# W_down weight sums: one pair of F tiles per gate/up pair, GpSimd's part tied to product ends, a new ring order

## The chip, the cores and the metric

The kernel runs on one core of a Trainium2 chip. The metric is the device time of one execution in microseconds (us), the median of several runs; lower is better. A ratio in this text is the mean time of one kernel's fast runs over that of the other kernel's fast runs of the same rounds, so it isn't quite the ratio of the medians that stand beside it. An interval is a 95% interval of such a ratio.

Short names: PE is TensorE (its matmuls), PEld its weight loads, DVE is VectorE, ACT is ScalarE, POOL is GpSimd, SP is the sequencer that issues nearly all DMAs, in program order.

## The reference, cut to what matters

The model is a linear-attention block and then a gated MLP, both with a layernorm in front. Only the MLP matters here (S = 2048 tokens, D = 1024, F = 3584, bf16):

```python
gate = x @ W_gate                  # D x F
up   = x @ W_up                    # D x F
h    = relu(gate) * up
out  = residual + h @ W_down       # F x D
```

The kernel does it in two passes of 1024 tokens. A pass has a gate/up stage, in 14 *pairs* of F tiles, and a *down* stage. Both use a fast matrix product of seven block products (P1 to P7, in the order P1, P5, P6, P2, P7, P3, P4) instead of eight; parts of the down stage use it at two levels. Fewer matmuls are paid for with sums of weight blocks. Those of W_down are made once, in pass 0, beside the gate/up matmuls, written to scratch in HBM and read back by both down stages.

## The kernel before: the parts that matter

For each pair `q` a raw 512 KB block of W_down is loaded into one of two buffers (`wraw`). VectorE makes four sums of it (`wd_sums`), then, for every two pairs, four second-level sums (`wl_sums`, two halves); GpSimd makes four more straight from the raw blocks (`raw`). All three are stored.

```python
def wd_sums(q):                       # VectorE, 4 subtractions from wraw into wsum, then a store (t_scr)
    ...
def wl_sums(m):
    def half(i): ...                  # VectorE, 2 + 2 subtractions from wsum; then a store (l_scr)
    def addw(j, x, y):                # GpSimd
        PL.add("pool", lambda e: e.tensor_tensor(..., op=ALU.subtract), reads=x[1] + y[1], ...)
    def raw():
        addw(0, ...); addw(2, ...); addw(1, ...); addw(3, ...)
        dma(..., "st_wm_%d" % m)      # the store (l_scr)
```

A pair calls lists of such functions at fixed places of its seven products: `mid[0]` before P2, `mid[2]` inside P2, `mid[3]` before P3, `mid[1]` before P4. Late layernorm tiles of the next pass also run here, in pairs 3 to 10.

```python
wt_at = {q: [q] for q in range(NPAIR - 1)}
wt_at[NPAIR - 2].append(NPAIR - 1)          # pair 12 makes the sums of pairs 12 and 13
...
for x in wt_at.get(q, []):
    mid[1 if q == 0 else 0].append(lambda x=x: wd_sums(x))
    if x % 2 == 1:
        w0_, w1_, wr_ = wl_sums(x // 2)
        mid[1].append(w0_); wl_q.append(w1_); mid[0].append(wr_)
        # then the raw loads of the next two pairs, also in mid[0]
if q not in wt_at:                           # pair 13: no sums, all seven ring loads
    mid[0] += wl_q + [load_wd_next] * NWS
```

The down stage reads its weights through a *ring* of seven slots. A load may start when its slot is free; from then on each finished product starts the load seven places ahead. Slots 0 to 3 lie over `wraw` and `wsum`, so they are free when the last sums are done. Slot 4 lies over GpSimd's sums, slots 5 and 6 over the late layernorm tiles, which are done two pairs before the end. At the end of every pair SP also issues two gate/up loads of 512 KB each.

Of the kernel before, what the change touches and what calls it, by code (L numbers as in the profile page):

```python
# [132 lines left out]
def bass_sequential_preLN__linear_attn_block__glu_gated_reglu__prompt_kernel(  # L133
# [72 lines left out]
    with es:  # L206
# [143 lines left out]
        def bank(b, w=512):  # L350
            return ps[:, b, 0:w]
# [100 lines left out]
        def flat(x):  # L452
            return [b for row in x for b in (flat(row) if isinstance(row, list) else [row])]
# [20 lines left out]
            b_.over = B_wo  # L474
        for b_ in B_wd[0:NWS - 3]:
            b_.over = B_wraw + flat(B_wsum)
        for b_ in flat(B_lsw):
            b_.over = flat(B_xnT) + flat(B_pqT)
        B_wd[NWS - 3].over = flat(B_lsw)
# [60 lines left out]
        def dma(slot, dst_ap, src_ap, name, reads=(), writes=(), eng="sp"):  # L540
            return PL.add(eng, lambda e: e.dma_start(dst_ap, src_ap), reads=reads, writes=writes, slot=slot,  # L541
                          name=name)
# [52 lines left out]
        for src in WSRC:  # L595
            if src[0] == "l":
                WLIST += [("l", src[1]) + x for x in LSRC]
            else:
                WLIST += [src + c for c in WCH]

        X_AT = [(NPAIR - 3) * 2 + i for i in range(NWX)]
        RING = [list(range(NWS))]
        RING.append([(len(WLIST) + i) % NWS for i in range(NWS)] +
                    [NWS + (NPAIR * 2 + x) % NWG for x in X_AT])

        def wd_slot(L):
# [57 lines left out]
        def wl_sums(m):  # L664
            z = m % 2
            no = len(L2O)
            oa = slice(L2O[0], L2O[-1] + 1)

            def wq_(k, h):
                return wsum[:, (2 * m + k) % NWR, oa, h * HNW:(h + 1) * HNW], \  # L670
                    [B_wsum[(2 * m + k) % NWR][o] for o in L2O]

            def t(j):
                return lsum[:, z, :, j, :], [B_lsum[z][j]]

            def add(j, x, y):
                PL.add("dve", lambda e: e.tensor_tensor(out=lsum[:, z, :, j, :], in0=x[0], in1=y[0],
                                                        op=ALU.subtract),
                       reads=x[1] + y[1], writes=[B_lsum[z][j]], name="WL%d_%d" % (j, m))

            def half(i):
                if i == 0:
                    add(0, wq_(0, 1), wq_(0, 0))
                    add(2, wq_(1, 1), wq_(0, 1))
                else:
                    add(1, wq_(1, 1), t(0))
                    add(3, wq_(1, 0), t(1))
                    dma(sl_ls[z], l_v[:, 0:no, :, m, :], lsum[:, z], "st_wl_%d" % m, reads=B_lsum[z],
                        writes=[B_lscr[m]])
            def wr(k, h):  # L690
                return wraw[:, (2 * m + k) % NWR, 1, NW + h * HNW:NW + (h + 1) * HNW], [B_wraw[(2 * m + k) % NWR]]

            def addw(j, x, y):
                PL.add("pool", lambda e: e.tensor_tensor(out=lsw[:, z, j, :], in0=x[0], in1=y[0], op=ALU.subtract),
                       reads=x[1] + y[1], writes=[B_lsw[z][j]], name="WM%d_%d" % (j, m))

            def raw():
                def t_(j):
                    return lsw[:, z, j, :], [B_lsw[z][j]]
                addw(0, wr(0, 1), wr(0, 0))  # L700
                addw(2, wr(1, 1), wr(0, 1))
                addw(1, wr(1, 1), t_(0))
                addw(3, wr(1, 0), t_(1))
                dma(sl_lw[z], l_v[:, no, :, m, :], lsw[:, z], "st_wm_%d" % m, reads=B_lsw[z], writes=[B_wscr[m]])
            return [lambda: half(0), lambda: half(1), raw]

        def mm(out_ap, lhsT, rhs, start, stop, reads, bbuf, name, skip=False):
# [600 lines left out]
        def strassen_pair(ps_, q, fill, mid):  # L1308
# [16 lines left out]
            def s_blk(i):  # L1325
                return (lambda kk: Ssum[:, i, kk, :]), [B_S[i]]

            def w_blk(w, k, h):
                return (lambda kk: wring[:, iw[w], k * KH + kk, h * P:(h + 1) * P]), [B_w[iw[w]]]

            def t_blk(w, j):
                return (lambda kk: Tring[:, kt[w], j, kk, :]), [B_T[kt[w]][j]]

            def prod(w, b, st_, mov, start, name):
                (sf, sr), (mf, mr) = st_, mov
                for kk in range(KH):
                    mm(bank(b), sf(kk), mf(kk), start and kk == 0, kk == KH - 1, sr + mr, B_bank[b],
                       "%s%s_%d_%d" % (name, "gu"[w], ps_, q), skip=True)

            def add_s5(dst, src, bsrc, w, bdst, name):  # L1340
                PL.add("dve", lambda e: e.tensor_tensor(out=dst, in0=src, in1=ftmp[:, w, :], op=ALU.add),  # L1341
                       reads=[bsrc, B_s5[w]], writes=[bdst], name=name)
# [29 lines left out]
            fillin(1)  # L1372
            for w in range(2):
                prod(w, BB[w], t_blk(w, 2), s_blk(2), False, "P7")
                add_s5(c22[:, w, :], bank(BB[w]), B_bank[BB[w]], w, B_c22[w], "c22")
            relu(c22[:, 0, :], c22[:, 0, :], [], B_c22[0], "rl22")
            for f_ in mid[3]:
                f_()
            for w in range(2):
                prod(w, BC_[w], w_blk(w, 1, 1), s_blk(3), False, "P3")  # L1380
                add_s5(c12[:, w, :], bank(BC_[w]), B_bank[BC_[w]], w, B_c12[w], "c12")
                if w == 0:
                    mul(hh[:, f2, SBW:2 * SBW], c22[:, 0, :], c22[:, 1, :], B_c22, B_hh[f2][1], "hh22")
# [25 lines left out]
        def down_pass(ps_, fill):  # L1409
# [253 lines left out]
            def at(pi, ci, *fs):  # L1663
                post.setdefault((pi, ci), []).extend(fs)
# [26 lines left out]
            for i, f_ in enumerate(sg4 + sg3):  # L1691
                at(4, i // 2, f_)
            order = (2, 3, 0, 1)
            at(5, 0, *[lambda j=j: add_h(V_, B_V, 1, 0, j) for j in order], *[lambda j=j: p_22(j) for j in range(STB)],
               lambda: e_u5(0), lambda: e_u5(1))
            at(5, 1, lambda: e_u5(2), lambda: e_u5(3))
            at(5, 4, st_flush)
            for f_, places in fill:
                at(*places, f_)
# [194 lines left out]
        wl_q = []  # L1894
        ln_q = []
        LQ = 3
        wt_at = {q: [q] for q in range(NPAIR - 1)}
        wt_at[NPAIR - 2].append(NPAIR - 1)

        for p_ in range(NPASS):  # L1900
            fill = []
            for q in range(NPAIR):
                if q + 1 < NPAIR:
                    fill = fill + t_sums((p_ * NPAIR + q + 1) * 2)
                if q > 0:
                    hh_sums(q - 1)
                mid = [[], [], [], []]
                if p_ == 0:
                    mid[2] += ln_q
                    ln_q.clear()  # L1910
                    if q == LQ - 1:
                        mid[2] += [lambda: late_load(0), lambda: late_load(1)]
                    if LQ <= q < LQ + TPP:
                        m_, sq_, n_ = late_steps(q - LQ)
                        mid[2].append(m_)
                        mid[3].append(sq_)
                        ln_q.append(n_)
                    for x in wt_at.get(q, []):
                        mid[0] += wl_q
                        wl_q.clear()  # L1920
                        mid[1 if q == 0 else 0].append(lambda x=x: wd_sums(x))
                        if x % 2 == 1:
                            w0_, w1_, wr_ = wl_sums(x // 2)
                            mid[1].append(w0_)
                            wl_q.append(w1_)
                            mid[0].append(wr_)
                            for z in (x + 1, x + 2):
                                if z < NPAIR:
                                    mid[0].append(lambda z=z: load_wraw(z))
                    if q not in wt_at:  # L1930
                        mid[0] += wl_q + [load_wd_next] * NWS
                        wl_q.clear()
                strassen_pair(p_, q, fill, mid)
                if p_ == 1 and q >= NPAIR - 3:
                    load_wd_next()
                    load_wd_next()
            assert not fill
            hh_sums(NPAIR - 1)
            late = []
            if p_ + 1 < NPASS:  # L1940
                slots_ = [(0, 1), (0, 3), (2, 0), (2, 1), (2, 2), (2, 3), (4, 1), (4, 2)]
                late = [(lambda t=t: late_t(t), slots_[t]) for t in range(TPP)]

                def nxt_t():
                    claim(flat(B_T[0:2]), B_sgo)
                    claim(flat(B_T[2:4]), B_sgo + B_dsum)

                def nxt_s():
                    claim(B_S, [B_D2])
                ss = s_sums()  # L1950
                ts = t_sums((p_ + 1) * NPAIR * 2)
                late += [(nxt_t, (3, 1))] + [(ts[i], (3, 2 + i)) for i in range(4)]
                late += [(nxt_s, (4, 4))] + [(ss[i], (6, (0, 0, 1, 2)[i])) for i in range(4)]
            down_pass(p_, late)
# [53 lines left out]
```

## Time and profile before

| | before |
|---|---|
| median (first 3 runs) | 736.23 us (735.11 to 737.95) |
| span of the profiled run | 734.9 us |
| PE busy | 98% |
| a gate/up pair with no wait | 12.08 us for 56 matmuls of 512 columns |
| pairs of pass 0 that cost more | 12.23, 12.53 and 13.18 us |
| down stage of pass 0 (from the last pair's P4) | 82.53 us |

The page of before, parts 1 (busy time, share of the span, instructions) and 4 (the chain that ended last, share by engine), one line of each:

```profile
PE 720.8 (98%) x4253; PEld 363.2 (49%) x4311; DVE 561.6 (76%) x976; ACT 352.0 (48%) x614; POOL 103.7 (14%) x169
...
PE 82%; DVE 9%; DMA 3%; issue 2%; ACT 2%; SPq 1%; POOL 1%; POOLq 0%; DVEq 0%; ACTq 0%
```

TensorE sets the pace. What a change of the sums can reach is the time in which PE waits. Before, the view of waits for PE from 225 us to the end (who waited for whom: us in total, times, longest) has three lines:

```profile
PE ps L710 <- DVE RE L1341: 1.6, 2, 1.1
PE ps L710 <- DVE RAB L1423: 1.0, 1, 1.0
PE ps L710 <- DMA RW<-in_B_W_down_dram: 0.4, 1, 0.4
```

The first is at 266 and 388 us in the gate/up stage; the other two come near 470 us, at the end of the down stage. Three us in all. The cause of the longest stall in the gate/up stage is seen in the timeline of before (start, duration, engine, line, operation, tile out <- in, forms, count; in brackets the idle time in front of it and what ended it):

```profile
377.88 0.84 POOL L694 TENSOR_TENSOR RAB<-RW 128x256 f16<-128x256 bf16 x1 [10.43 <-DMA RW<-in_B_W_down_dram]
...
380.60 1.15 DVE L1289 TENSOR_TENSOR RO<-RWG 128x1024 f16<-128x1024 bf16 x1
...
383.21 3.01 DVE L655 TENSOR_TENSOR RW<-RW 128x512 f16<-128x512 bf16 x8
...
388.30 1.67 PE L710 MATMUL ps<-RH,RO 128*128 128x512 bf16 x7 [1.14 <-DVE RE L1341]
```

Eight first-level sums in a row (L655) took VectorE 3.01 us, where a pair with four takes 1.55 us when nothing slows them. A T sum (L1289) took 1.15 us beside GpSimd; undisturbed it takes 0.68 us. PE then waits 1.14 us for VectorE's addition from PSUM.

### The profile page before, as it was taken

The page shows a single profiled execution, that of the slowest core. Times are in us where ns is not written, and L with a number is a line of the kernel's source. Part 1 is how long each engine was busy: PE and PEld are TensorE (multiplying, and loading weights), DVE is VectorE, ACT ScalarE, POOL GpSimd, SP SyncE. Part 2 cuts the span into 40 slices and gives each one's busy share as a digit, 9 for nine tenths or more (in the row PEclk, how much of TensorE's full clock was granted, in tenths as well). Part 3 has the DMA queues.
Part 4 walks back from the last instruction along what each step waited for, and adds up shares of the span by engine and source line. Part 5 has one row for each costly group of instructions (what it writes and reads, how often), then busy time and mean ns, then how long its engine had stood idle before and what let it go on. Part 6 is the DMA issues. An engine that isn't in the chain of part 4 may idle for free.

```text
span 734.9 us, 11505 instructions
## 1 busy us (share of the span) xinstructions
PE 720.8 (98%) x4253; PEld 363.2 (49%) x4311; DVE 561.6 (76%) x976; ACT 352.0 (48%) x614; POOL 103.7 (14%) x169
## 2 busy tenths in 40 slices
PE   8999999999999999999999999999999999999998
PEld 3444444344444444444444666754444444447766
DVE  7878877898775999898997769865757575667594
ACT  4877666764832456777754100135454544521000
POOL 1311100000450112132320003400000000000052
PEclk9999999999999999999999999999999999999999
DMA  9644154024999889888969999982323242327892
GB/s 313 202 91 83 29 142 157 3 30 75 214 228 260 234 258 272 241 243 256 300 198 305 318 247 336 311 263 79 101 71 109 63 116 58 100 92 245 246 314 87
DMA packets 191880, 133.93 MB, mean 182 GB/s; under 512 B 51664, under 2 KB 173776, under 8 KB 191824
## 3 DMA queue, kind: packets, MB, share of 16 engines
q1 hardware_dynamic: 191152, 132.54, 63.6%
q8 instruction: 34, 0.56, 0.3%
q10 hardware_dynamic: 672, 0.66, 0.3%
q14 instruction: 22, 0.18, 0.1%
HBM read 96.47 MB, written 25.17 MB: 166 GB/s over the span
## 4 chain that ended last, share of the span: by engine, by line
PE 82%; DVE 9%; DMA 3%; issue 2%; ACT 2%; SPq 1%; POOL 1%; POOLq 0%; DVEq 0%; ACTq 0%
PE ps L710 82%; DMA RW<-in_B_W_down_dram 1%; DVE RAB L796 1%; DVE RE L1171 1%; ACT RX L789 1%; DMA RX<-h_scr 1%; DVE st L724 1%; DMA RAB<-RXH 1%; DVE RX L793 1%; SPq L541 1%; DVE RX L1012 1%; DVE RO L1289 1%; POOL rstd L734 0%; DVE RW L906 0%; ACT ps L715 0%
## 5 line engine op out<-in xcount | busy, mean ns | idle before, releaser
L715 ACT ACTIVATE ps<-ps 128x512 f32<-128x512 f32 x172 | 100.1, 582 | 213.5 <-PE ps L710 162.0
L710 PE MATMUL ps<-RC,RO 128*128 128x512 f16 x672 | 154.3, 379 | 0.0
L710 PE MATMUL ps<-RH,RWG 128*128 128x512 bf16 x447 | 105.6, 379 | 0.1
L710 PEld LDWEIGHTS ps<-RC,RO 128*128 128x128 f16 x672 | 65.7, 98 | 79.5 <-ACT ps L715 0.5
L1345 DVE TENSOR_TENSOR RAB<-ps,RAB 128x512 bf16<-128x512 f32 x56 | 38.6, 689 | 71.9 <-PE ps L710 71.9
L710 PE MATMUL ps<-RC,RWG 128*128 128x512 f16 x320 | 76.8, 379 | 0.3 <-ACT ps L715 0.3
L1341 DVE TENSOR_TENSOR RE<-ps,RE 128x512 bf16<-128x512 f32 x112 | 74.2, 684 | 1.6 <-PE ps L710 0.7
L710 PEld LDWEIGHTS ps<-RH,RWG 128*128 128x128 bf16 x448 | 43.9, 98 | 52.6
L710 PE MATMUL ps<-RW,RAB 128*128 128x256 f16 (+3 forms) x412 | 66.8, 318 | 1.5 <-DVE RAB L1423 1.0
L1423 POOL TENSOR_TENSOR RE<-RE,RX 128x512 f32<-128x512 f32 x16 | 23.1, 1473 | 307.5 <-DMA RX<-h_scr 307.5
L715 ACT ACTIVATE RE<-RE 128x512 bf16<-128x512 bf16 x56 | 35.1, 627 | 65.0 <-DVE RE L1341 64.4
L710 PE MATMUL ps<-RH,RO 128*128 128x512 bf16 (+1 forms) x228 | 55.3, 379 | 3.0 <-DVE RE L1341 1.6
L710 PE MATMUL ps<-RW,RE 128*128 128x512 bf16 x243 | 56.6, 380 | 1.5 <-DVE RXH L1195 0.7
L710 PE MATMUL ps<-RAB 128*128 128x512 bf16 (+2 forms) x268 | 57.6, 351 | 0.4
L715 ACT ACTIVATE RE<-ps 128x512 f32<-128x512 f32 x64 | 37.6, 597 | 35.4 <-PE ps L710 35.0
L710 PEld LDWEIGHTS ps<-RW,RAB 128*128 128x128 bf16 (+1 forms) x414 | 40.4, 98 | 25.8 <-DVE RAB L1423 1.3
L710 PEld LDWEIGHTS ps<-RC,RWG 128*128 128x128 bf16 (+1 forms) x320 | 30.0, 98 | 40.2 <-ACT ps L715 6.2
L1289 DVE TENSOR_TENSOR RO<-RWG 128x1024 f16<-128x1024 bf16 x54 | 39.7, 736 | 4.7 <-DMA RWG<-in_B_W_up_dram 4.7
L1423 DVE TENSOR_TENSOR RE<-ps,RE 128x512 f32<-128x512 f32 x40 | 27.0, 687 | 18.9 <-PE ps L710 15.6
L715 ACT ACTIVATE RAB<-ps 128x512 bf16<-128x512 f32 x56 | 33.4, 596 | 14.7 <-PE ps L710 13.6
L710 PEld LDWEIGHTS ps<-RH,RO 128*128 128x128 f16 (+1 forms) x256 | 24.2, 98 | 31.8 <-DVE RE L1341 2.2
L710 PEld LDWEIGHTS ps<-RAB 128*128 128x128 bf16 (+1 forms) x274 | 26.3, 98 | 25.2 <-ACT RAB L856 1.1
(138 smaller groups left out, 994.0 us busy)
## 6 DMA issues: line engine op xcount, KB each, us to landing
RWG<-in_B_W_gate_dram SPq DMA_DIRECT2D x28, 512.0 KB, 5.0
RWG<-in_B_W_up_dram SPq DMA_DIRECT2D x28, 512.0 KB, 5.9
RW<-in_B_W_down_dram SPq DMA_DIRECT2D x14, 512.0 KB, 6.1
t_scr<-RW SPq DMA_DIRECT2D x14, 512.0 KB, 3.5
RE<-in_A_x_dram SPq DMA_DIRECT2D x23, 256.0 KB, 3.5
RW<-l_scr SPq DMA_DIRECT2D x13, 448.0 KB, 6.3
l_scr<-RX SPq DMA_DIRECT2D x7, 768.0 KB, 4.4
RW<-in_B_W_down_dram SPq DMA_DIRECT2D x12, 384.0 KB, 5.0
```

The costliest lines, as they stand in the source:

```text
L541: return PL.add(eng, lambda e: e.dma_start(dst_ap, src_ap), reads=reads, writes=writes, slot=slot, name=name)
L710: lambda e: e.matmul(out_ap, lhsT, rhs, start=start, stop=stop, skip_group_check=skip),
L715: PL.add("act", lambda e: e.activation(out=dst, in_=src, func=func), reads=reads, writes=writes, name=name)
L724: PL.add("dve", lambda e: e.bn_stats(out=st6[:, k, c * 6:(c + 1) * 6], in_=src_full[:, c * BCH:(c + 1) * BCH]), reads=[src_chunk_bufs[c]], ...
L789: PL.add("act", lambda e: e.activation(out=Et[:, k, :], in_=src, func=ACTF.Exp), reads=[src_buf], writes=[B_E[k]], name=name + "_exp")
L793: PL.add("dve", lambda e: e.tensor_scalar(out=Et[:, k, :], in0=Et[:, k, :], scalar1=1.0, scalar2=1e-6, op0=ALU.min, op1=ALU.add), reads=[] ...
L796: PL.add("dve", lambda e: e.scalar_tensor_tensor(out=dst_ap, in0=src, scalar=C1, in1=Et[:, k, :], op0=ALU.add, op1=ALU.max), reads=[src_bu ...
L1012: PL.add("dve", lambda e: e.tensor_tensor(out=s_, in0=p_, in1=s_, op=ALU.add), reads=[pb], writes=[sb_], name=name + "_add")
L1289: PL.add(eng, lambda e: e.tensor_tensor(out=tb(j, u), in0=f0(u), in1=f1(u), op=ALU.subtract), reads=[B_w[i + x] for x in r] + ([B_T[k + x] ...
L1341: PL.add("dve", lambda e: e.tensor_tensor(out=dst, in0=src, in1=ftmp[:, w, :], op=ALU.add), reads=[bsrc, B_s5[w]], writes=[bdst], name=name)
L1345: PL.add("dve", lambda e: e.tensor_tensor(out=dst, in0=a_, in1=b_, op=ALU.mult), reads=reads, writes=[wr], name=name)
L1423: PL.add(eng, lambda e: e.tensor_tensor(out=dst, in0=in0, in1=in1, op=op), reads=reads, writes=writes, name=name)
```

## The change

The intent: spread the sums evenly (pair 13 makes its own), keep GpSimd out of VectorE's way by letting each of its four subtractions start only at the end of a P7 or P3 product, when VectorE adds from PSUM, and make up for the later sums by filling the ring in the order in which slots come free (5, 6, 0, 1, 2, 3, 4). Four U5 additions of the down stage also move ahead of a wait. The core of the diff:

```diff
+        for b_ in B_wd[0:2]: b_.over = list(B_wraw)      # ring slots 0 and 1 wait for wraw alone
...
-        RING = [list(range(NWS))]
+        RING = [[NWS - 2, NWS - 1] + list(range(NWS - 2))]
...
             def addw(j, x, y):
                 PL.add("pool", ...,
-                       reads=x[1] + y[1], ...)
+                       deps=[PL.prog["pe"][-1]], reads=x[1] + y[1], ...)
-            def raw(): addw(0..); addw(2..); addw(1..); addw(3..); dma(.. "st_wm_%d")
+            def last():
+                addw(3, ...)
+                if m == NM - 1:
+                    load_wd_next()
+                    load_wd_next()
+                dma(.. "st_wm_%d")
+                ...load_wraw of the next two pairs, which stood in mid[0]
+            raw = [addw(0..), addw(2..), addw(1..), last]
...
                 prod(w, BB[w], t_blk(w, 2), s_blk(2), False, "P7")
+                run(mid[4], 1)
...
                 prod(w, BC_[w], w_blk(w, 1, 1), s_blk(3), False, "P3")
+                run(mid[4], 1)
...
-               lambda: e_u5(0), lambda: e_u5(1))
-            at(5, 1, lambda: e_u5(2), lambda: e_u5(3))
+               *[lambda j=j: e_u5(j) for j in range(STB)])
...
-        wt_at = {q: [q] for q in range(NPAIR - 1)}
-        wt_at[NPAIR - 2].append(NPAIR - 1)
+        wt_at = {q: [q] for q in range(NPAIR)}
...
-                            mid[0].append(wr_)
+                            mid[4] += wr_
-                    if q not in wt_at:
-                        mid[0] += wl_q + [load_wd_next] * NWS
+                    if q == NPAIR - 1:
+                        mid[0] = [load_wd_next] * 2 + mid[0]
+                        mid[1] += wl_q
                 strassen_pair(p_, q, fill, mid)      # its end: two gate/up loads
+                if p_ == 0 and q == NPAIR - 1:
+                    for _ in range(NWS - 4):
+                        load_wd_next()
```

More of the change, by code (lines that the diff above doesn't have):

```diff
@@ L476, in bass_sequential_preLN__linear_attn_block__glu_gated_reglu__prompt_kernel @@
             b_.over = B_wraw + flat(B_wsum)
+        for b_ in B_wd[0:2]:
+            b_.over = list(B_wraw)
         for b_ in flat(B_lsw):
@@ L601, in bass_sequential_preLN__linear_attn_block__glu_gated_reglu__prompt_kernel @@
         X_AT = [(NPAIR - 3) * 2 + i for i in range(NWX)]
-        RING = [list(range(NWS))]
-        RING.append([(len(WLIST) + i) % NWS for i in range(NWS)] +
+        RING = [[NWS - 2, NWS - 1] + list(range(NWS - 2))]
+        RING.append([RING[0][(len(WLIST) + i) % NWS] for i in range(NWS)] +
                     [NWS + (NPAIR * 2 + x) % NWG for x in X_AT])
@@ L694, in addw, with t_ @@
                 PL.add("pool", lambda e: e.tensor_tensor(out=lsw[:, z, j, :], in0=x[0], in1=y[0], op=ALU.subtract),
-                       reads=x[1] + y[1], writes=[B_lsw[z][j]], name="WM%d_%d" % (j, m))
-            def raw():
-                def t_(j):
-                    return lsw[:, z, j, :], [B_lsw[z][j]]
-                addw(0, wr(0, 1), wr(0, 0))
-                addw(2, wr(1, 1), wr(0, 1))
-                addw(1, wr(1, 1), t_(0))
+                       deps=[PL.prog["pe"][-1]], reads=x[1] + y[1], writes=[B_lsw[z][j]], name="WM%d_%d" % (j, m))
+            def t_(j):
+                return lsw[:, z, j, :], [B_lsw[z][j]]
+            def last():
                 addw(3, wr(1, 0), t_(1))
+                if m == NM - 1:
+                    load_wd_next()
+                    load_wd_next()
                 dma(sl_lw[z], l_v[:, no, :, m, :], lsw[:, z], "st_wm_%d" % m, reads=B_lsw[z], writes=[B_wscr[m]])
+                for q in (2 * m + NWR, 2 * m + NWR + 1):
+                    if q < NPAIR:
+                        load_wraw(q)
+            raw = [lambda: addw(0, wr(0, 1), wr(0, 0)), lambda: addw(2, wr(1, 1), wr(0, 1)),
+                   lambda: addw(1, wr(1, 1), t_(0)), last]
             return [lambda: half(0), lambda: half(1), raw]
@@ L1906, in bass_sequential_preLN__linear_attn_block__glu_gated_reglu__prompt_kernel @@
                     hh_sums(q - 1)
-                mid = [[], [], [], []]
+                mid = [[], [], [], [], []]
                 if p_ == 0:
@@ L1925, in bass_sequential_preLN__linear_attn_block__glu_gated_reglu__prompt_kernel @@
                             wl_q.append(w1_)
-                            mid[0].append(wr_)
-                            for z in (x + 1, x + 2):
-                                if z < NPAIR:
-                                    mid[0].append(lambda z=z: load_wraw(z))
-                    if q not in wt_at:
-                        mid[0] += wl_q + [load_wd_next] * NWS
+                            mid[4] += wr_
+                    if q == NPAIR - 1:
+                        mid[0] = [load_wd_next] * 2 + mid[0]
+                        mid[1] += wl_q
                         wl_q.clear()
                 strassen_pair(p_, q, fill, mid)
+                if p_ == 0 and q == NPAIR - 1:
+                    for _ in range(NWS - 4):
+                        load_wd_next()
                 if p_ == 1 and q >= NPAIR - 3:
```

## The prediction

> **What bounds the kernel.** TensorE. The page gives PE 98% of the 734.9 us span, and the chain of work that ended last is 82% PE. In the windows of the gate/up stage a pair of F tiles takes 12.08 us for 56 matmuls of 512 columns, which is the same 12.08 us in pairs where nothing is late, so PE runs back to back. The view of waits, taken stretch by stretch for PE, leaves little after 225 us: 0.5 us at 266 and 1.1 us at 388 (both for VectorE's additions from PSUM, RE line 1341), then 1.0 us at 470 (VectorE, RAB line 1423) and 0.4 us at 472 (the W_down load). Measured start to start, pairs cost 12.23, 12.53 and 13.18 us instead of 12.08: 0.15 + 0.45 + 1.1 = 1.7 us lost in pass 0, and 1.4 us in its down stage. 3.1 us is all that the change can reach.
>
> **What it removes.**
> 1. The pair before the last did two W_down sums: in the timeline eight additions in a row, 3.0 us, at 383.2. VectorE was busy 12.97 of that pair's 13.18 us. One set moves into the last pair, where VectorE idles 3.0 us at 394. The 1.1 us stall should vanish.
> 2. GpSimd's four subtractions (0.67 to 1.11 us each) ran beside VectorE's SBUF-to-SBUF work. There VectorE's operations stretched: 0.41 to 0.89 us (W_down sums), 0.68 to 1.16 us (T sums). I count about 8 us of stretch over the pass (mean minus median, times count). The Trainium skill, "SBUF — State Buffer", section "SBUF: two separate sides", calls the shared port pair an exclusive lock, taken by a VectorE op with two SBUF inputs against a GpSimd op that reads SBUF; the stretched durations agree. The change releases each subtraction at the end of a P7 or P3 product, when VectorE adds from PSUM. So the 0.15 and 0.45 us go too. Little of the 8 us is on the critical path.
> 3. Four U5 additions go ahead of VectorE's 1.94 us wait for GpSimd at 464. The two outputs behind come about 1.3 us earlier; the 1.0 us stall goes.
>
> **What it adds or moves.** The same operations and bytes. Raw W_down loads are issued about 5 us later in the odd pairs; with 5 to 6 us to landing they arrive just when VectorE wants them (slack about 1 us). Ring loads: two start about 3 us earlier, but the next two wait for GpSimd's last subtraction (about 401, wanted from 407), the last three for VectorE's last sums (about 404 to 408, wanted from 412 to 415). Loads land in 5 to 8 us here, DMA is near full (windows 400 to 420: 325 GB/s), so waits of 0.5 to 1 us on W_down loads may appear at the start of the down stage. At 472 the load was issued at 464.0 and took 8.0 us: without the 1.0 us stall PE reaches it sooner and may wait longer for it, so that stall is only partly won.
>
> **Sum.** -1.7 (gate/up), about -0.5 of 1.4 (end of down), about +0.6 (start of down): -1.6 us. Predicted 734.6 us, range 732.4 to 736.8. Faster by over 2%: 0.01; within 2%: 0.985; slower: 0.005.
>
> **What would show it.** All 14 pairs of pass 0 at 12.08 us; W_down sums and T sums near 0.42 and 0.68 us in maximum too; no PE wait on line 1341; no PE wait on RAB at 470, but a longer one on the W_down load; PE waits on RW loads near 407 to 416, if any.
>
> **What would make it wrong.** VectorE waiting for the later raw loads in every second pair, which would stall PE up to six times (+3 us); a late ring costing more than 2 us; or the load after 464 coming earlier, for the full 3.1 us.

## The result, and the profile after

| | before | after |
|---|---|---|
| median of 6 runs each | 736.35 us | 739.69 us |
| range | 735.11 to 737.95 | 739.38 to 740.76 |
| ratio | | 1.0049 [1.0034, 1.0063] |
| span of the profiled run | 734.9 us | 739.0 us |

After is slower by half a per cent: small, but clear of noise, and outside the predicted range. The page of after, the same two lines:

```profile
PE 724.8 (98%) x4311; PEld 362.7 (49%) x4311; DVE 555.8 (75%) x976; ACT 352.3 (48%) x614; POOL 103.3 (14%) x169
...
PE 75%; DVE 8%; DMA 8%; issue 2%; SPq 2%; POOL 2%; ACT 2%; POOLq 0%; DVEq 0%; ACTq 0%
```

PE is still 98% busy, but on the chain DMA went from 3% to 8%. (The PE counts differ because some matmul records are missing from a trace, not in the kernel.) The view of waits for PE from 225 us to the end of after:

```profile
PE ps L718 <- DMA RW<-in_B_W_down_dram: 1.9, 1, 1.9
PE ps L718 <- DVE RE L1349: 1.5, 2, 1.3
PE ps L718 <- DMA RW<-t_scr: 0.8, 1, 0.8
PE ps L718 <- DVE RAB L1433: 0.6, 2, 0.4
PE ps L718 <- DMA RE<-in_B_W_down_dram: 0.5, 1, 0.5
```

A wait can understate a delay here, as matmul ends are modelled: the 12.23 us pair of before shows no wait. So I read the start times of fixed matmuls from PE's timeline and subtracted them. The marks are: P4 of the first pair, P4 of the last pair, the first matmul of the down stage's second direct product, the first matmul of pass 1, the end. Only the four stretches between them are compared: in the profiled runs the 241 to 243 us in front, which no edit here touches, differ by up to 1.9 us. The stages scatter too, and each kernel has one profile: after, a1, a2, d1 and d3 below have the same gate/up code up to the last pair, and show 159.08 to 159.66 us. After's profile is of its slowest run (740.76 us), so its stages add up to more than the medians differ by.

| us | gate/up, 13 pairs | start of down | rest of down | pass 1 to the end |
|---|---|---|---|---|
| before | 158.81 | 24.51 | 58.02 | 252.0 |
| after | 159.43 | 27.88 | 57.82 | 252.2 |
| difference | +0.62 | +3.37 | -0.20 | +0.2 |

Two things went wrong, one in each of the first two columns.

**Gate/up.** Nine of the 13 steps from pair to pair cost 12.08 to 12.10 us in after, also the one that had cost 13.18. But the four pairs behind an odd pair with a late layernorm tile cost 12.51, 13.52, 12.29 and 12.29 us. The timeline of after around the worst one, engines sorted in here by time:

```profile
300.28 1.55 POOL L696 TENSOR_TENSOR RAB<-RW 128x256 f16<-128x256 bf16 x2 [6.83 <-issue]
301.93 0.30 POOL L771 TENSOR_SCALAR s<-s 128x1 f32<-128x1 f32 x1
303.12 0.19 POOL L774 TENSOR_TENSOR s<-s 128x1 f32<-128x1 f32 x1 [0.89 <-ACT RE L756]
303.39 0.55 POOL L781 TENSOR_TENSOR s<-s,neghalf 128x1 f32<-128x1 f32 x1
304.04 0.80 POOL L1248 TENSOR_SCALAR s<-s 128x1 f32<-128x1 f32 x1
304.81 1.57 POOL L696 TENSOR_TENSOR RAB<-RW,RAB 128x256 f16<-128x256 bf16 x2
306.41 0.37 SPq L543 DMA_DIRECT2D l_scr<-RAB  x1
306.82 1.11 SPq L543 DMA_DIRECT2D RW<-in_B_W_down_dram  x2
...
312.67 1.56 DVE L657 TENSOR_TENSOR RW<-RW 128x512 f16<-128x512 bf16 x4 [3.01 <-DMA RW<-in_B_W_down_dram]
...
316.08 1.90 PE L718 MATMUL ps<-RH,RO 128*128 128x512 bf16 x8 [1.27 <-DVE RE L1349]
```

GpSimd takes its operations in program order here: its four layernorm operations stand between the second and the third subtraction and wait for ScalarE (303.12), and the third subtraction starts only behind them, at 304.81. The last subtraction ends at 306.4, the raw loads go out at 306.8, VectorE waits 3.0 us for them, and PE waits for VectorE. Before, the raw loads of the same pair went out 3.1 us ahead of its P4, not 4.3 us behind it:

```profile
299.25 1.87 SPq L541 DMA_DIRECT2D RW<-in_B_W_down_dram  x2
```

**Start of the down stage.** The DMA issues of after, from its timeline:

```profile
389.82 2.27 SPq L543 DMA_DIRECT2D RE<-in_B_W_down_dram  x2
394.14 0.37 SPq L543 DMA_DIRECT2D t_scr<-RW  x1
402.17 0.90 SPq L543 DMA_DIRECT2D RW<-in_B_W_down_dram  x2
403.11 0.49 SPq L543 DMA_DIRECT2D l_scr<-RAB  x1
404.15 0.37 SPq L543 DMA_DIRECT2D l_scr<-RX  x1
404.61 2.79 SPq L543 DMA_DIRECT2D RWG<-in_B_W_gate_dram  x1
407.51 1.00 SPq L543 DMA_DIRECT2D RWG<-in_B_W_up_dram  x1
408.60 2.37 SPq L543 DMA_DIRECT2D RW<-in_B_W_down_dram  x1
```

SP issues nothing from 394.5 to 402.2 us: it stands at the ring load that waits for GpSimd's last subtraction, which ends at 402.1 (SP's view of waits gives 7.6 us for it). Then six transfers come at once, and the fifth ring load (slot 2, the third over the W_down buffers) is issued at 408.60 and lands at 415.3, 1.9 us too late. Before issued in the same place, in its timeline:

```profile
394.02 0.37 SPq L541 DMA_DIRECT2D l_scr<-RX  x1
394.56 3.83 SPq L541 DMA_DIRECT2D RW<-in_B_W_down_dram  x4
398.49 0.43 SPq L541 DMA_DIRECT2D RAB<-in_B_W_down_dram  x1
...
```

The last two of its seven ring loads follow at 399.09 and 399.81.

The same is seen in the view of windows (time, length, busy time and count of PE, PEld, DVE, ACT and POOL, then granted clock, DMA busy share and GB/s). Before:

```profile
395.00:400.00 5.00, 5.00 (x25) 2.29 (x24) 2.56 (x4) 1.81 (x3) 0.00 (x0) 1.00 0.95 292
400.00:405.00 5.00, 4.95 (x24) 2.29 (x24) 4.25 (x10) 1.23 (x2) 0.00 (x0) 1.00 1.08 338
```

After:

```profile
395.00:400.00 5.00, 5.00 (x25) 2.25 (x23) 1.78 (x3) 2.32 (x5) 0.96 (x2) 1.00 0.58 200
400.00:405.00 5.00, 5.00 (x24) 2.25 (x23) 4.79 (x10) 1.32 (x3) 1.72 (x3) 1.00 0.32 88
405.00:410.00 5.00, 5.00 (x25) 2.28 (x24) 4.65 (x12) 0.00 (x0) 0.00 (x0) 1.00 1.11 335
```

In these 10 us before moves (292 + 338) x 5 us = 3.15 MB and after (200 + 88) x 5 us = 1.44 MB. Straight behind, after is back at 335 GB/s with the engines full.

How much could it catch up? The Trainium skill, "DMA: Bandwidth & Descriptors", section "Where 436 GB/s comes from", gives about 358 GB/s as the HBM limit of one core, half of 716 GB/s for two. This trace doesn't agree: before moves 395 GB/s from 445 to 450 us and 367 from 472 to 485. So what the start of the down stage can take is read from its own windows, from 4 us behind the last pair's P4 to the second direct product. Before and after:

```profile
404.39:424.90 20.51, 20.41 (x143) 13.99 (x143) 16.55 (x26) 3.33 (x6) 0.00 (x0) 1.00 1.08 308
405.13:429.01 23.88, 21.02 (x145) 13.76 (x143) 18.32 (x29) 3.34 (x6) 0.00 (x0) 1.00 1.14 302
```

The rate is nearly the same (a2_sums_early and d3_defer_far, below, show 306 and 303), the bytes aren't: 308 GB/s x 20.51 us = 6.3 MB and 302 GB/s x 23.88 us = 7.2 MB. No run shows more than 320 there (b2_one_sum), so there is little with which to catch up. The 0.9 MB more at 305 GB/s are an estimated 2.9 us of the 3.4 us lost.

### The profile page after: what moved, and what is told of

Same layout as the page of the kernel before. It is cut to its first block, busy times and chain, and to the rows that moved or that the text cites. A ratio compares the mean times of both kernels' runs of the same rounds, so it can differ in the third digit from the quotient of the medians.

```text
span 739.0 us, 11580 instructions
## 1 busy us (share of the span) xinstructions
PE 724.8 (98%) x4311; PEld 362.7 (49%) x4311; DVE 555.8 (75%) x976; ACT 352.3 (48%) x614; POOL 103.3 (14%) x169
## 4 chain that ended last, share of the span: by engine, by line
PE 75%; DVE 8%; DMA 8%; issue 2%; SPq 2%; POOL 2%; ACT 2%; POOLq 0%; DVEq 0%; ACTq 0%
PE ps L718 75%; SPq L543 2%; DMA RW<-in_B_W_down_dram 2%; DMA RX<-h_scr 1%; DMA RAB<-in_A_wqkv_dram 1%; DVE RAB L804 1%; DMA RE<-in_B_W_down_dram 1%; POOL RE L1433 1%; DMA RW<-t_scr 1%; DVE RE L1179 1%; DVE RX L801 1%; DVE RX L1020 1%; DMA RE<-RE 1%; DMA RAB<-RXH 1%; ACT RX L797 1%
## 5 line engine op out<-in xcount | busy, mean ns | idle before, releaser
L718 PE MATMUL ps<-RW,RAB 128*128 128x256 f16 (+3 forms) x404 | 63.1, 313 | 1.9 <-DMA RW<-in_B_W_down_dram 1.9
L718 PE MATMUL ps<-RH,RO 128*128 128x512 bf16 (+1 forms) x256 | 61.2, 379 | 1.6 <-DVE RE L1349 1.5
L718 PE MATMUL ps<-RAB 128*128 128x512 bf16 (+1 forms) x258 | 54.3, 350 | 0.3
L718 PEld LDWEIGHTS ps<-RW,RAB 128*128 128x128 f16 (+1 forms) x404 | 39.5, 98 | 23.4 <-DMA RW<-in_B_W_down_dram 2.4
L1297 DVE TENSOR_TENSOR RO<-RWG 128x1024 f16<-128x1024 bf16 x54 | 36.9, 684 | 4.5 <-DMA RWG<-in_B_W_up_dram 4.5
L718 PEld LDWEIGHTS ps<-RW,RE 128*128 128x128 bf16 x256 | 24.0, 98 | 28.9 <-DVE RXH L1203 1.2
```

Of the source, the lines that this page charges most:

```text
L718: lambda e: e.matmul(out_ap, lhsT, rhs, start=start, stop=stop, skip_group_check=skip),
L1297: PL.add(eng, lambda e: e.tensor_tensor(out=tb(j, u), in0=f0(u), in1=f1(u), op=ALU.subtract), reads=[B_w[i + x] for x in r] + ([B_T[k + x] ...
```

## The experiments

Every experiment's kernel gave correct results. Each row has its own before, run on the same chip.

| run | median | its before | ratio and interval | gate/up | start of down | rest of down |
|---|---|---|---|---|---|---|
| after | 739.69 | 736.35 | 1.0049 [1.0034, 1.0063] | 159.43 | 27.88 | 57.82 |
| a1_wd_first | 741.47 | 736.19 | 1.0074 [1.0061, 1.0086] | 159.66 | 28.17 | 57.49 |
| a2_sums_early | 737.25 | 736.19 | 1.0023 [1.0011, 1.0036] | 159.08 | 25.27 | 57.44 |
| a3_ln_behind | 738.05 | 736.19 | 1.0024 [1.0010, 1.0037] | 157.12 | 28.71 | 57.37 |
| b1_u5 | 736.03 | 736.19 | 0.9999 [0.9986, 1.0012] | 159.13 | 24.51 | 57.46 |
| a4_untied | 736.75 | 736.00 | 1.0013 [1.0001, 1.0026] | 157.27 | 26.51 | 57.88 |
| a5_both | 735.37 | 736.00 | 0.9990 [0.9977, 1.0002] | 157.12 | 24.88 | 57.51 |
| b2_one_sum | 734.62 | 736.00 | 0.9985 [0.9973, 0.9998] | 157.71 | 24.74 | 57.59 |
| c1_best | 734.74 | 736.00 | 0.9979 [0.9965, 0.9993] | 157.12 | 24.51 | 57.62 |
| d1_defer_gate_up | 742.81 | 737.38 | 1.0065 [1.0044, 1.0087] | 159.46 | 24.85 | 61.42 |
| d2_old_ring | 736.25 | 737.38 | 0.9979 [0.9956, 1.0002] | 157.13 | 26.24 | 57.58 |
| d3_defer_far | 737.87 | 736.86 | 1.0020 [1.0006, 1.0033] | 159.15 | 24.53 | 58.06 |
| c2_best_defer | 735.23 | 736.86 | 0.9977 [0.9965, 0.9990] | 157.13 | 24.51 | 57.85 |

The three stage columns are of the one profiled run. The stretch behind them lies between 251.6 and 252.3 us in all of these, so nothing is decided there.

### a1_wd_first: the order of the queue

```diff
                 strassen_pair(0, NPAIR - 1)
-                    (end of the pair) 2 gate/up loads
-                3 x load_wd_next()
+                    (end of the pair) 3 x load_wd_next(), then 2 gate/up loads
```

> The kernel after, with one edit: the last three W_down loads of the first ring filling are issued ahead of the two gate/up loads at the end of the last pair, not behind them. After stalls PE 1.9 us at 415.3 for the third ring slot, whose load was issued at 408.6, 4 us behind its data being free (VectorE's last sum, 404.1). Theory Q (queue order): the load goes out near 404.6, lands near 410 to 411 and PE does not wait for it at 413; the waits at 425 and 427 shrink too: 2 to 3 us faster than after, so 737. Theory D (the DMA engines are simply full there, 310 to 346 GB/s in the slices, and the same bytes come either way): the wait moves to another load and the time stays within 0.7 us of after. Theory F (the slots come free too late): stays at after as well, as no slot comes free earlier.

The fifth ring load did go out early, at 405.15 us, and PE didn't wait for it any more. Nothing was won: the start of the down stage took 28.17 us, against 27.88. The waits moved to the loads behind. The view of waits for PE from 225 us on, its DMA lines:

```profile
PE ps L718 <- DMA RE<-l_scr: 1.2, 1, 1.2
PE ps L718 <- DMA RW<-l_scr: 1.0, 2, 0.7
PE ps L718 <- DMA RW<-t_scr: 0.8, 1, 0.8
PE ps L718 <- DMA RAB<-l_scr: 0.6, 1, 0.6
```

Theory Q falls. Theory D is right that the wait moves to other loads, but by the medians a1 lies outside its 0.7 us. That the median lies 1.8 us above that of after isn't explained by any stage, and the two intervals overlap; I claim only that it isn't faster.

### a2_sums_early: the second-level sums early

```diff
-   mid[1] of the last pair (behind P3): 4 second-level sums and their store
+   mid[0] of the last pair, right behind the 4 first-level sums
```

> The kernel after, with one edit: in the last pair the four second-level W_down sums follow right behind the four first-level sums (VectorE idles 3.8 us there, from 394.1), not behind product P3. The third to fifth ring slots are then free at about 397, not 404, and the store of these sums no longer holds the DMA queue to 404. Theory F (the slots come free late): the gate/up loads and the three ring loads move about 1 to 2 us earlier and the waits of 1.9 and 0.8 us shrink by that: 1 to 2.5 us faster than after. Theory Q: the three loads still stand behind the store that waits for GpSimd (402) and behind the two gate/up loads, so less than 1 us. Theory D: within 0.7 us of after.

The start of the down stage fell from 27.88 to 25.27 us, and the ratio from 1.0049 to 1.0023. By the medians, 2.4 us, it is the upper end of what theory F expected; by the ratios it is 1.9 us. Where the time came from isn't quite what theory F says, though: the fifth ring load went out at 405.25, 4.8 us behind the last pair's P4; in a1 it went out 3.3 us behind it (405.15), and that won nothing. What differs is that the 768 KB store of these sums now goes out at 395.2, into the hole: 302 GB/s from 395 to 400 us where after has 200. That suggested theory H of the later runs.

### a3_ln_behind: layernorm behind the subtractions

```diff
             late layernorm tile, pairs 3 to 10:
                 mid[3]: ScalarE's square
-                mid[3]: GpSimd's four small operations      (between subtractions 2 and 3)
+                mid[1]: GpSimd's four small operations      (behind subtraction 4)
```

> The kernel after, with one edit: in the pairs that do a late layernorm tile, GpSimd's four small layernorm operations are queued behind its four W_down subtractions, not between the second and the third. In after these four small operations wait for ScalarE's square (275.7 to 280.2), so the third and fourth subtraction end at 281.8 where product P3 ended at 278.0, the raw W_down loads go out at 282.2, and VectorE waits for them four times, 8.6 us in all, up to 3.0; PE pairs then cost 12.51 and 13.52 us. Theory L (these operations hold the loads): the loads go out 2 to 2.5 us earlier in four odd pairs, as they do in the pair at 376.9 where no layernorm stands between; VectorE's waits fall under 1.5 us in all; every pair of pass 0 costs 12.08 us; 1.5 to 2.3 us faster than after. Theory T (the tie to P7 and P3 alone makes the loads too late): VectorE still waits over 5 us and the time stays within 0.7 us of after.

All 13 pair steps of pass 0 took 12.08 or 12.09 us, 157.12 us in all, 2.3 us less than after and 1.7 less than before. The view of VectorE's waits from 240 to 405 us, after:

```profile
DVE RAB L1353 <- PE ps L718: 13.4, 11, 3.8
DVE RW L657 <- DMA RW<-in_B_W_down_dram: 8.6, 4, 3.0
```

and a3_ln_behind, where the second line is gone:

```profile
DVE RAB L1361 <- PE ps L718: 20.5, 18, 3.8
DVE RE L1357 <- PE ps L718: 0.3, 2, 0.2
```

Theory L holds and theory T falls: the tie alone doesn't make the raw loads too late. The start of the down stage took 28.71 us, 0.8 more than after. The hole is still there, and PE waited 2.1 us for the same ring load, but what is new is the clock. Behind this wait the granted TensorE clock was 0.50 from 415.0 to 418.4 us, an estimated 1.7 us lost; at full clock the start would have taken about 27.0 us. The one other profile with such a stretch before PE's work ends is d1, behind a wait of 2.6 us; behind the waits of 1.9 us in after and a1 the clock stayed at 1.00. a3's profile is of its slowest run; whether its other runs had such a stretch isn't known.

### b1_u5: the U5 additions alone

```diff
-   at(5, 0, ..., e_u5(0), e_u5(1));  at(5, 1, e_u5(2), e_u5(3))
+   at(5, 0, ..., e_u5(0), e_u5(1), e_u5(2), e_u5(3))
```

> The kernel before, with one part of the change alone: all four U5 additions ahead of VectorE's wait for GpSimd in the down stage. My theory: PE's 1.0 us stall for VectorE's output goes, but the next unit's W_down load, issued in the same place, then holds PE for longer than 0.4 us: 0 to 0.7 us faster than before. The rival is that the part is worth its full 1.0 to 1.4 us, so the loss of the whole change is that much larger elsewhere; or that it is worth nothing.

The rest of the down stage took 57.46 us, not 58.02, and the times can't tell it from before (0.9999). PE's wait for VectorE fell from 1.0 to 0.3 us, and the wait for a load rose from 0.4 to 0.6 us. That fits the theory, but doesn't show it: b2_one_sum, below, lacks this edit, and its rest of the down stage is as short (57.59 us), with a wait for VectorE of 0.5 us. Half a us is within the scatter of single profiles, so what this part is worth isn't shown.

### a4_untied: the tie taken off (from a3_ln_behind)

```diff
-   addw: deps=[PL.prog["pe"][-1]], reads=...
+   addw: reads=...
```

> The kernel of a3_ln_behind with the tie taken off: GpSimd's four subtractions no longer wait for the end of a P7 or P3 product. If the tie does what it was meant for, VectorE's SBUF operations stretch again (W_down sums up to 0.9 us, T sums up to 1.1 us, as in before) by some 0.5 to 1.5 us in the odd pairs. My theory: PE does not notice or hardly notices, as the first-level sums are now spread over the pairs and the raw loads go out earlier still: pairs stay within 12.08 to 12.5 us, and the time within 0.5 us of a3_ln_behind. The rival: the stretch alone delays PE as at 266 us in before, by 0.4 us or more in several pairs, so 1 us or more slower than a3_ln_behind.

The tie does what it was meant for: untied, VectorE's T sums of the first form take 821 ns in the mean instead of 685, W_down sums 443 instead of 420. But PE lost only 0.15 us by it, in one pair. (Before lost 0.6 us in two; without the tie 0.45 us of this is still gone, and no run shows which part of the change took it away.) And the tie costs more than that elsewhere. Untied, GpSimd makes its last four subtractions at 377.8 to 382 us, as soon as the raw blocks have landed; tied, at 397.3 to 400.6 us. So the third and fourth ring load go out at 392.27 instead of 400.63 us, and the start of the down stage takes 26.51 instead of 28.71 us. Of this 2.2 us an estimated 1.7 are the clock in a3's profile, which leaves 0.5 for the tie. By the ratios a4 is 0.8 us faster than a3, more than the 0.5 us of the theory, though the two intervals overlap. Its DMA issues in the timeline:

```profile
391.80 0.37 SPq L543 DMA_DIRECT2D t_scr<-RW  x1
392.27 1.56 SPq L543 DMA_DIRECT2D RW<-in_B_W_down_dram  x2
```

### a5_both: a2 and a3 together

> The kernel after with the edits of a2_sums_early and a3_ln_behind together. If these two causes are the whole loss and add: 2.4 + 1.6 us faster than after, so 735.5 to 736 beside a before of 736.2, all pairs of pass 0 at 12.08 us and waits of about 1.3 us left in the down stage. If there is a further cause in the change, it stays over 737.

Gate/up 157.12 us, start of down 24.88, ratio 0.9990: the two causes together account for the loss. It is 0.0059 below the ratio of after; a2 and a3 alone are 0.0026 and 0.0025 below it (each against its own before).

### b2_one_sum: the even sums alone, on the kernel before

```diff
-        wt_at: pair 12 makes the sums of pairs 12 and 13
+        wt_at: pair q makes the sums of pair q
         pair 13, mid[0]:
-            wl_q, 7 x load_wd_next()
+            wd_sums(13), both halves of wl_sums(6), GpSimd's four, 7 x load_wd_next()
```

> The kernel before with one part of the change alone, one W_down sum set per pair, but with all sums of the last pair and all seven ring loads at the place where before has its ring loads (product P2 of the last pair); GpSimd untied and the old ring order. My theory: the 1.1 us stall at 388 goes, the 0.15 and 0.45 us at 254 and 266 stay, the start of the down stage waits at most 0.5 us as the first ring load goes out 2 to 3 us later than in before but none is behind the gate/up loads: 0.5 to 1.1 us faster than before. The rival: any sum in the last pair, wherever placed, frees the ring too late, and the down stage loses over 1 us as in after: same as before or slower.

Gate/up fell by 1.1 us to 157.71: the 13.18 us pair is gone, the 12.22 and 12.54 us pairs stay. The start of the down stage is 0.2 us longer. The ratio is 0.9985. So the first part of the change is worth having where the last pair's sums stand early enough: VectorE idles there (in before 3.0 us at 394). By the ratios it is 1.1 us faster than before, most of what c1_best below wins with all parts (1.5 us); the intervals don't tell the two apart.

### c1_best: all repairs on the kernel after

```diff
    a3_ln_behind, and for the last pair:
-   mid[0]: 2 ring loads, wd_sums;  mid[4]: GpSimd's four, 2 ring loads;  mid[1]: wl_sums;  end: 3 ring loads
+   mid[0]: 2 ring loads, wd_sums, wl_sums, GpSimd's four, 2 + 3 ring loads
```

> The kernel after with a3_ln_behind's edit, and with all sums of the last pair (VectorE's eight, GpSimd's four) and the last five ring loads at product P2 of the last pair, so that no DMA hole is left between 395 and 405 us (after moves 200 and 88 GB/s in these two slices, before 292 and 338). My theory: all pairs at 12.08 us (1.7 us less than before), no wait of over 0.5 us at the start of the down stage, and about 1 us of wait at its end: 734 to 735, 1.2 to 2.2 us faster than before. If the hole is not what costs, the down stage stays 2 us or more longer than that of before, and the time over 737.

Every pair 12.08 or 12.09 us, the start of the down stage back at 24.51 us, 734.74 us, ratio 0.9979. By the two ratios it is faster than before by 0.2% and than after by 0.7%. The hole is gone, in the windows of c1_best:

```profile
395.00:400.00 5.00, 4.95 (x24) 2.24 (x23) 3.72 (x7) 1.73 (x3) 1.69 (x3) 1.00 0.99 291
400.00:405.00 5.00, 5.00 (x25) 2.25 (x23) 4.19 (x10) 0.60 (x1) 0.00 (x0) 1.00 1.08 319
```

### d1_defer_gate_up and d3_defer_far: bytes or lateness

What is the hole's harm: that slots are filled late (theory S), or that idle DMA time is bytes lost from a stage that has none to spare (theory H)? Both runs are after, with nothing moved earlier; only the two gate/up loads of 512 KB are put off.

```diff
     end of the last pair of pass 0:
-        2 x load_w_next()
+    d1: during the second direct product of the down stage     d3: in the first pair of pass 1
```

> The kernel after, with one edit: the two gate/up loads (1.0 MB) at the end of the last pair of pass 0 are issued some 20 us later, in the down stage's second direct product; they are not needed before the third pair of the next pass. The sums, the ring loads' places and the 8 us in which the DMA queue issues nothing (394.5 to 402.2) stay as in after. Theory H (the idle DMA time is lost throughput: after moved 1.7 MB less than before between 395 and 405 us, and the down stage then waits for bytes, in whatever order they stand): taking 1.0 MB out of the crowded time gives back about 3 us of the 3.2 that the down stage lost at 320 GB/s: 2 to 3 us faster than after, 737 to 737.7. Theory S (the sums come too late and hold the slots, bytes do not matter): the third ring slot's load may go out at 404.6 but, as in a1_wd_first, this wins nothing: within 0.7 us of after.

On its face d1 refuted theory H: 742.81 us, ratio 1.0065, on a chip with much noise (its before ranges to 741.58). The stages tell more. The start of the down stage was repaired, from 27.88 to 24.85 us. But the rest grew by 3.6 us, to 61.42, with one wait that after doesn't have, in the timeline of PE:

```profile
449.91 3.13 PE L718 MATMUL ps<-RW,RAB 128*128 128x256 f16 x14 [2.61 <-DMA RW<-t_scr]
```

Behind this wait the clock was 0.50 from 449.5 to 452.9 us: the 14 matmuls take 2.94 us to the next ones, where after takes 1.53. So 2.6 us of the growth are the wait, and the clock, 1.4 us, covers the rest. The two loads went out at 435.3 and 443.4 us, and the debt came due again there. So the deferral had to reach beyond the down stage, which d3 does.

> d1_defer_gate_up took the two waits at 415 and 427 away, and a new one of 2.6 us came at 450 for a second-pass load, behind the 1.0 MB that it had put off by only 20 us. Here the same two loads are put off past the whole down stage, to the first pair of the next pass, where the DMA share is 0.3; they are needed from the second pair of it on. All else is as in after. Theory H (the down stage moves more bytes than it has DMA time for, so each idle stretch before it is paid later, wherever the queue happens to be short): now the 1.0 MB is really gone from it, so the down stage falls from 85.7 to about 83 us and the time by 2.5 to 3 us against after: ratio to before 1.001 to 1.002. Theory S (late sums hold the slots, bytes do not matter): the down stage stays over 85 us and the ratio near 1.005.

(In after the DMA share of that first pair is 0.72; 0.31 is that of the next one. The loads did no harm there.) The start took 24.53 us, the rest 58.06, together 82.6. The ratio was 1.0020, at the slow end of what theory H gave: 2.1 us below after by the ratios, 3.1 by the stages. The hole is still there in its windows, and the sums are as late as in after:

```profile
395.00:400.00 5.00, 5.00 (x25) 2.24 (x24) 1.38 (x2) 2.31 (x5) 0.67 (x1) 1.00 0.76 253
400.00:405.00 5.00, 5.00 (x25) 2.25 (x23) 4.73 (x10) 1.79 (x3) 2.01 (x3) 1.00 0.21 48
```

Theory H holds for the down stage and theory S falls: the late sums cost nothing once 1.0 MB less has to be moved by it. One rival isn't separated by a run: the two loads also took SP 3.8 us to issue in after. That the DMA engines were full in that stretch (share 1.14) speaks for the bytes.

### d2_old_ring and c2_best_defer

d2 is c1_best with slots filled 0 to 6 and all seven loads behind the sums (slots 0 and 1 wait for `wsum` again, too):

```diff
-        RING = [[NWS - 2, NWS - 1] + list(range(NWS - 2))]
+        RING = [list(range(NWS))]
-        mid[0] = [load_wd_next] * 2 + mid[0]
+        mid[0] += [load_wd_next] * 2
```

> The kernel of c1_best with the old ring order (slots 0 to 6 in turn, all seven loads behind the sums of the last pair, none ahead of them). It asks what the new ring order is worth where nothing else is late. My theory: two loads are issued 3 to 4 us later and still land before they are wanted at 401 to 403, or hold PE for up to 0.5 us: 0 to 0.7 us slower than c1_best, a ratio to before of 0.998 to 0.999. The rival: the new order is what makes one sum per pair possible at all, then 1.5 us or more slower than c1_best.

The ratio is that of c1_best, 0.9979, but the interval is 0.0046 wide. In the profiled run, its slowest, the start of the down stage is 1.7 us longer (26.24 against 24.51), with waits of 0.8 us and less; the first load went out at 398.04, behind GpSimd's tied subtractions. In b2_one_sum the old order cost 0.2 us with the subtractions untied (first load at 395.6). What the new order is worth under the tie stays open.

> c1_best with the same deferral. Its down stage has 0.26, 0.34 and 0.23 us of waits left, two of them for loads. Theory H: these two go, 0 to 0.6 us faster than c1_best (ratio to before about 0.997); no more is to be had there, as TensorE then runs without a gap. If DMA bytes do not matter, it equals c1_best (0.998).

0.9977 against c1_best's 0.9979: no difference. The waits at the end of the down stage didn't go: two for loads remain, 0.33 and 0.65 us. So theory H's expectation of up to 0.6 us isn't borne out here.

## Why the prediction was wrong

The prediction's form was a sum: "-1.7 (gate/up), about -0.5 of 1.4 (end of down), about +0.6 (start of down): -1.6 us". Measured, by the stages: +0.6, -0.4, +3.4.

1. **What bounds the kernel: right.** PE's waits were all there was to win. c1_best runs gate/up at 157.12 us, exactly 13 x 12.08 to 12.09.
2. **The even sums, "the 1.1 us stall should vanish": right.** That pair took 12.09 us in after, and b2_one_sum shows the part alone.
3. **"So the 0.15 and 0.45 us go too": right as to the number, the cause shown in part.** Those two pairs took 12.09 us. But with the tie alone taken off (a4_untied) only 0.15 us came back; what else took 0.45 us away stays open. W_down sums are at 426 ns at most in after; in before they reached 889. The tie's other side was missed: it moves GpSimd's last subtractions some 20 us later than GpSimd would do them untied (a4_untied). The prediction took the tie to be free but for later loads.
4. **The raw loads, "issued about 5 us later in the odd pairs ... slack about 1 us": wrong, the first step that failed.** Relative to the pair's P4, before issues them 3.1 us ahead (371.78 and 374.90; the first record of this P4, 0.22 us, is missing), after 1.7 us behind in the one odd pair at that end of the pass with no layernorm in it (378.67 and 376.95): 4.8 us later, as predicted. In the four odd pairs that carry a layernorm tile, after issues them 4.3 us behind (306.82 and 302.56). The other 2.5 us are GpSimd's four layernorm operations, which stand in its queue between the subtractions. The prediction named a VectorE wait for raw loads as what would make it wrong, but gave it no cost in the sum; -1.7 became +0.6. a3_ln_behind shows it: with only these four operations moved, -1.7 is what is measured.
5. **The end of the down stage, -0.5: the number came out, the cause isn't shown.** From the marks at 459.56 and 463.89, first matmul of the third two-level product, to pass 1 it is 23.36 us before and 22.94 after. But b2_one_sum, without the U5 edit, also has 22.94 (458.64 to 481.58), and c1_best, with it, 22.96. So this hit may be luck.
6. **The start of the down stage, +0.6: the term that was most mis-sized.** The mechanism was in the prediction: loads wait for GpSimd's last subtraction "about 401" (402.2), the last three come "404 to 408" (408.6 to 411.8), "waits of 0.5 to 1 us ... may appear". It was costed load by load, as latency: each lands in 5 to 8 us, when is it wanted? It should have been costed as throughput. The prediction itself noted that the DMA engines are near full from 400 to 420; then 8 us with an idle queue can't be made up, and 1.7 MB less moved from 395 to 405 us is, at 335 GB/s, an estimated 5 us of debt, of which PE paid 3.4 (the 0.9 MB still owed 4 us behind P4 are 2.9 us of it). a1 (order: nothing), a2 (store into the hole: -2.6 us) and d3 (1.0 MB taken out: -3.4 us) show it.

## What to carry to other kernels

When a stage is short of DMA time, cost a late release not by the one transfer it delays but by the bytes the queue doesn't move while it stands still: reordering the queue won't bring them back, filling the gap or taking bytes out of the stage will. Before tying an engine's work to a moment, look at what else stands in that engine's queue between the pieces, and at what its completion frees. And when an experiment shifts a wait rather than removing it (d1), compare the stages, not only the total, and look at the granted clock of each: 3.4 us at half clock stand in the stage times of a3 and d1.

## What the Trainium skill lacked or had wrong

- "SBUF — State Buffer", section "SBUF: two separate sides", states the exclusive lock between VectorE and GpSimd but gives no size for such subtractions. Here a VectorE subtraction of 128x512 went from 0.41 to as much as 0.89 us beside GpSimd subtractions of 0.67 to 1.11 us, and back to 0.43 at most when the change kept them apart; PE lost 0.15 us by it in one pair of a4_untied, and at most 0.6 us in two of before's pairs.
- "DMA: Bandwidth & Descriptors", section "Issuing engines are not separate DMA queues", calls the sequencer's time to start a DMA usually small beside the DMA itself. It can be a third of it: the same kind of 512 KB gate load took SP 0.37 us to issue at 388.42 (4.9 us to landing) and 2.79 us at 404.61 (8.1 us) in after, and what stands behind it in the queue waits. Full engines alone don't explain this, as their busy share was 1.13 from 388 to 390 us and 1.00 from 404 to 406; four transfers had been issued in the 2.5 us in front of the slow one. The cause stays open.
- No page that I read has a way to cost an idle DMA stretch in a stage that is short of DMA time; the numbers here are 1.7 MB less moved in 10 us and 3.4 us lost.
